# Routing attention and MLP mixer: the third pair's routing in PSUM bank 5, and softmax denominators finished two pairs at a time

## The chip, the cores and the metric

The kernel runs on one core of a Trainium2 chip. The metric is the device time of one execution in microseconds (us). The time before the change is 791.66 us, the median of three runs (791.56 to 792.14).

Five engines are spoken of: TensorE (PE, with its weight loads in rows of their own, PEld), VectorE (DVE), ScalarE (ACT), GpSimd (POOL) and SyncE (SP, which here only issues DMAs). TensorE writes its results to PSUM, eight banks of 2 KB for each of 128 partitions; all else lies in SBUF, in one array that the program calls `arena`.

## The reference

Four batches, eight heads, a sequence of 768 and 64 elements per head. Attention is limited to keys of the same cluster, and its output goes through an MLP mixer. Cut to what matters:

```python
B, H, S, D = q.shape                       # 4, 8, 768, 64
q_assign = argmax(q_n @ c_n.T); k_assign = argmax(k_n @ c_n.T)   # 16 centroids per head
mask = q_assign[:, :, :, None] == k_assign[:, :, None, :]
scores = np.where(mask, q @ k.T / sqrt(D), -1e9)
attn = exp(scores - max); attn = attn / (sum(attn) + 1e-9)
x = (attn @ v) as (B, S, H * D)            # (4, 768, 512)

xt = x.transpose(0, 2, 1)
h = np.maximum(xt @ w_tok1, 0.0) @ w_tok2  # d_tok = 256
u = x + h.transpose(0, 2, 1)
out = u + np.maximum(u @ w_ch1, 0.0) @ w_ch2   # d_ch = 1536
```

## The kernel before, in words

**How the order comes about.** The kernel first writes its whole work down as a list of operations with the engines that may do each, a cost for each engine, and keys for what it reads and writes (`Program.add`, L89): grains of SBUF, and PSUM banks as `("ps", n)`. `Program.plan` (L152) then makes one order out of it. TensorE's operations keep the order in which they were written down; each other engine takes, of what is ready, what is due first. Some operations have an earliest time: each of the 31 pieces of weights that DVE rounds may be loaded from 9 + 10 n us on (`START`, `STEP`, L1356). So a change of one cost, one key or one operation can move many instructions on all engines but TensorE.

**The attention stage.** The 32 heads are worked on as 16 pairs, four pairs to a batch; `pair(m)` (L1317) writes down one pair:

- `scores(m)` (L1161): 12 chunks. Chunk n writes banks 2s and 2s+1 with s = n % 3, one bank per head, so three chunks use banks 0 to 5 in turn. Each is a plain product in float32 and a mask product in bfloat16 added to it. ScalarE takes the exponential of each chunk out of PSUM (L1205).
- `join_qk`, `part_qk` and `load_qkr` prepare q and k of later pairs: ScalarE takes their 16-bit halves apart and joins them (L875), and SP's queue transposes them by DMA (L910).
- `route(m, bk)` (L1079): four matmuls of q and k against the centroids into bank `bk`, then on DVE a transpose out of that bank (L1098), a maximum (L1099), a comparison and a transpose back (L1103), and on ScalarE L1108, which makes the bfloat16 mask rows. They go through DRAM to form the mask M of the pair. Inside `pair(m)` stands `route(m + 2, 0)` for the pairs 1 to 13, into bank 0. The third pair's routing, `route(2, 0)`, is written down at the end of pair 0, behind `finish_x(0, 5, 0)` and thus right ahead of the scores of pair 1.
- `values(m, i)` (L1249): exp times v into banks 6 and 7, six steps, by the matmuls of L1238.
- `add_up(m)` (L1213): DVE adds the exponentials of a pair up (four additions of 1536 elements per partition, a fifth in ten of the pairs) for the denominators.
- `sums(m, bk)` (L1263): a product with ones gives the denominators in bank 5 (bank 4 for the last pair). It is called in the next pair, behind its second step of values.
- `finish_x(m, bk, part)` (L1278): part 0 transposes banks 6 and 7 into x (L1285). Part 1 transposes the denominators out of their bank into `denT` (L1292), clamps the 12 numbers (L1295), inverts them (L1302) and multiplies the 768 elements of the pair in x by them (a `tt`, L885).

**Fillers.** Between these DVE rounds the mixer's weights (`weight_round`, L1349: L1369, L1373, L1376, L1379 and a `tt`) and makes sums of them (`channel_weights`, L1426, which writes them to the DRAM array `wd`, L1487). TensorE does not need these until the mixer.

**The mixer.** Behind the last pair come `token1` (L1565), `token2` (L1610), `x_into_u` (L1652), and then the channel products (`product`, L1708), each split into seven half-size products, with sums before (`combine`, L1687, by DVE or GpSimd) and additions out of PSUM behind them by DVE. Meanwhile the weights are loaded once more and their range is checked (L1884, L1908).

**Helpers.** Most operations go through short helpers, so one line of the profile stands for many: `mm` L846 for matmuls, `copy` L865 and L867, `halves` L875, `tt` L885, `relu` L892, `dma` L905, `transpose` L910.

Of the kernel before, what the change touches and what calls it, by code (L numbers as in the profile page):

```python
# [14 lines left out]
ALU = mybir.AluOpType  # L15
# [3 lines left out]
B, H, S, D = 4, 8, 768, 64  # L19
C = 16  # L20
P = 128
NJ = S // P
# [8 lines left out]
HS = HJ * P  # L31
# [692 lines left out]
def kernel(  # L724
# [26 lines left out]
    nc = tc.nc  # L751
    g = Program()
    res = ctx.enter_context(ExitStack())
    arena = res.enter_context(tc.tile_pool(name="arena", bufs=1)).tile(
        [P, 206 * 256], F32, name="arena"
    )
    ps = res.enter_context(tc.tile_pool(name="ps", bufs=1, space=bass.MemoryType.PSUM)).tile(
        [P, 8, 512], F32, name="ps"
    )
# [8 lines left out]
    def buf(kb, shape, dt=F32):  # L768
        return Buf(arena, int(kb * 256), shape, dt)
# [10 lines left out]
    low = Buf(arena, 644, [1])  # L780
    wsum = Buf(arena, 704, [2, NWP])
    araws = [buf(at, [768, 2], U32) for at in (75, 3)]
    rcps = [Buf(arena, 384 + 32 * i, [2, NJ]) for i in range(2)]
    dall = Buf(arena, 448, [NP, 2, NJ])

    qks = [buf(3 + 6 * i, [2, NJ, 2, D]) for i in range(2)]
# [5 lines left out]
    msc0 = Buf(arena, 332, [2, 2])  # L792
    exs = [buf(48 + 6 * i, [2, S]) for i in range(6)] + [buf(96, [2, S])]
    es = [buf(84 + 6 * i, [2, S]) for i in range(2)]
    denT = buf(105, [HS])
    okb = buf(131.5, [HS])
    rt = [buf(106.5 + 1.5 * i, [HS]) for i in range(3)]

# [13 lines left out]
    xs = [buf(158 + 12 * b, [NJ, DM]) for b in range(B)]  # L812
# [27 lines left out]
    def bank(*i):  # L840
        return [("ps", n) for n in i]
# [41 lines left out]
    def tt(dst, a, b, op, n, rd, wr, engines=("DVE",)):  # L883
        def fn(e):
            (nc.vector if e == "DVE" else nc.gpsimd).tensor_tensor(out=dst, in0=a, in1=b, op=op)  # L885

        return g.add({e: cost(e, n) for e in engines}, fn, rd, wr)
# [10 lines left out]
    def vec(fn, c, rd, wr, early=0.0, after=0.0):  # L898
        return g.add({"DVE": c - 0.08}, lambda e: fn(), rd, wr, after=after, early=early)
# [36 lines left out]
    def load_v(m, after=0.0):  # L936
        b, hp = divmod(m, H // 2)
        t = vs[m % 3]
        dma(
            t.ap.rearrange("p h j d -> p h (j d)"),  # L940
            v[b, 2 * hp : 2 * hp + 2].rearrange("h (p j) d -> p h (j d)", p=P),
            [], t.k(), 384, 1536, after,
        )
# [92 lines left out]
    def turn_qk(m, banks, parts=range(3)):  # L1036
        src, T = qks[m % 2], Ts[m % 3]
        for n in parts:
            bk = banks[n]
            for i in range(4):  # L1040
                a, j = divmod(4 * n + i, NJ)
                a = 1 - a
                turn(
                    ps[:, bk, i * P : (i + 1) * P],
                    src.ap[:, a, j].rearrange("p h d -> p (h d)"),
                    [("qk", m % 2, a, 0), ("qk", m % 2, a, 1)] + src.rows(a, a + 1), bank(bk),
                )

            copy(
                T.ap[:, 4 * n : 4 * n + 4].rearrange("p a t -> p (a t)"), ps[:, bk], 512,  # L1050
                bank(bk), T.rows(4 * n, 4 * n + 4),
            )
# [15 lines left out]
    def join_qk(m):  # L1068

        T = Ts[m % 3]  # L1070
        dst = T.ap.bitcast(U16).rearrange("p a (t two) -> p a t two", two=2)
        for n in range(2):
            for r in range(0, NQK, NJ):
                halves(
                    dst[:, r : r + NJ, :, n], qkt[n].ap[:, r : r + NJ], S,
                    qkt[n].k() + [("exps", m - 2)], T.rows(r, r + NJ), kind="JOIN16",
                )
# [135 lines left out]
    def add_up(m):  # L1213
        st = unit[m]
        for n in range(2):
            a = es[n]
            x, y, z = st[HJ * n : HJ * n + HJ]
            tt(a.ap, x.ap, y.ap, ALU.add, 2 * S, x.k() + y.k(), a.k())
            tt(a.ap, a.ap, z.ap, ALU.add, 2 * S, a.k() + z.k(), a.k())
        a, b = es[1], es[0]  # L1220
        if FOLD[m] == "V":
            tt(a.ap, a.ap, b.ap, ALU.add, 2 * S, a.k() + b.k(), a.k())
        if FOLD[m] != "T":
            return

        def fn(e):
            nc.gpsimd.dma_start(
                a.ap.rearrange("p h t -> p (h t)"), b.ap.rearrange("p h t -> p (h t)"),
                accum_op=ALU.add,
            )  # L1230

        g.add({"POOL": 1.0}, fn, a.k() + b.k(), a.k(), (2.2 * 768 * 1024, 6144))
# [16 lines left out]
    def values(m, i):  # L1249
        V, ex = vs[m % 3], unit[m][i]  # L1250
        mms(
            [
                (
                    ps[32 * gr : 32 * gr + 32, 6 + h, c * HS // 2 : (c + 1) * HS // 2],
                    V.ap[:, h, i, 32 * c : 32 * c + 32], tokens(ex.ap[:, h], gr),
                    i == 0 and c == 0, i == NJ - 1, (0, 32 * gr),
                )
                for h in range(2) for c in range(2) for gr in range(4)
            ],
            1.29, V.k() + ex.k(), bank(6, 7), (P, 32),  # L1260
        )

    def sums(m, bk):  # L1263
        first = 0 if FOLD[m] == "-" else 1
        for n in range(first, 2):
            mms(
                [
                    (
                        ps[32 * gr : 32 * gr + 32, bk, 0:HS], ones.ap,
                        tokens(es[n].ap.rearrange("p h t -> p (h t)"), gr), n == first, n == 1,  # L1270
                        (0, 32 * gr),
                    )
                    for gr in range(4)
                ],
                0.645, es[n].k() + ones.k(), bank(bk), (P, 32),
            )

    def finish_x(m, bk, part):  # L1278
        b, hp = divmod(m, H // 2)
        x, rcp = xs[b], rcps[m % 2]  # L1280
        cols = slice(hp * P, (hp + 1) * P)
        xk = x.rows(0, NJ, hp * P, (hp + 1) * P)
        if part == 0:
            vec(
                lambda: nc.vector.transpose(  # L1285
                    out=x.ap[:, :, cols].rearrange("p j (c d) -> p c j d", d=32),
                    in_=ps[:, 6:8, 0:HS],
                ),
                0.96, bank(6, 7), xk,
            )  # L1290
            return
        vec(lambda: nc.vector.transpose(out=denT.ap, in_=ps[:, bk, 0:HS]), 0.57, bank(bk), denT.k())  # L1292

        def den():
            nc.vector.tensor_scalar(  # L1295
                out=dall.ap[:, m].rearrange("p h j -> p (h j)"),
                in0=denT.ap.rearrange("p (n r) -> p n r", r=32)[:, :, 0],
                scalar1=SUM_LO / 2, scalar2=2 * SUM_HI, op0=ALU.max, op1=ALU.min,
            )

        vec(den, 0.2, denT.k(), [("dall", m)])
        vec(lambda: nc.vector.reciprocal(out=rcp.ap, in_=dall.ap[:, m]), 0.2,  # L1302
            [("dall", m)], rcp.k())
        xv = x.ap[:, :, cols].rearrange("p j (h d) -> p j h d", h=2)
        tt(
            xv, xv,
            rcp.ap.rearrange("p h j -> p j h").unsqueeze(3).to_broadcast([P, NJ, 2, D]),
            ALU.mult, S, xk + rcp.k(), xk,
        )

    def next_qk(m):
        if m + 3 < NP:
            part_qk(m + 3)
            if m + 4 < NP:
                load_qkr(m + 4)

    def pair(m):  # L1317
        scores(m)
        if m >= 1 and m + 2 < NP:
            join_qk(m + 2)  # L1320
        if m:
            next_qk(m)
        for i in range(NJ):
            if i == 3 and m == 0:
                turn_qk(2, (1, 2, 3))
            if i == 4 and 1 <= m < NP - 2:
                route(m + 2, 0)
            if i == 1:
                if m:
                    sums(m - 1, 5)  # L1330
                    finish_x(m - 1, 5, 1)
                add_up(m)
            values(m, i)
        if m == NP - 1:
            sums(m, 4)
        finish_x(m, 5, 0)
        if m == NP - 1:
            finish_x(m, 4, 1)
        if m == 0:
            load_v(2)  # L1340
            route(2, 0)
            next_qk(m)
        if m + 3 < NP:
            load_v(m + 3)
# [620 lines left out]
    for m in range(NP):  # L1965
        pair(m)
# [78 lines left out]
```

## Time and profile before

| what | value |
|---|---|
| median of three runs | 791.66 us |
| profiled execution | 791.57 us |
| its span in the trace | 789.7 us |
| mean granted TensorE clock | 0.998 |
| PE busy | 778.3 us (99%) |
| DVE busy | 677.9 us (86%) |
| ACT busy | 460.5 us (58%) |
| POOL busy | 190.1 us (24%) |
| PEld busy | 462.6 us (59%) |
| moved by DMA | 143.68 MB, 182 GB/s in the mean |

The span is the time from the first to the last instruction in the trace; the execution's own time has 1.9 us more. "Busy" is the time in which an engine carries out an instruction other than register, branch, semaphore and DMA-issuing ones. In a row of the timeline stand the start, the duration, the engine, the line of the kernel, the operation, what it writes and reads, and how many instructions of one kind the row takes together; in brackets the idle time ahead of it and what ended it. Rows of groups have a total and a mean in ns. SPq is SP's queue of DMA issues.

### The profile page before, as it was taken

Reading aid. Unit: us, or ns where it says so; the run is one execution under the profiler, and the core shown is the slowest. Engines: PE = TensorE matmul, PEld = TensorE weight load, DVE = VectorE, ACT = ScalarE, POOL = GpSimd, SP = SyncE. Lnnn points to the kernel's source line nnn. Section 1 sums busy time; section 2 is a strip of 40 time slices with the busy share of each in tenths; the row PEclk is TensorE's granted clock in tenths of the full one; section 3 lists DMA queues with packets and bytes.
Section 4 is the critical chain, followed back from the end, with each engine's and each line's share of the span. In section 5 each row is a group of like instructions: output and inputs, shape, how many; then the busy total and the mean of one; then the engine's idle time right before and its main releaser. Section 6 shows DMA issues by size and latency. Waiting matters only on the chain.

```text
span 789.7 us, 15348 instructions
## 1 busy us (share of the span) xinstructions
PE 778.3 (99%) x5975; PEld 462.6 (59%) x5975; DVE 677.9 (86%) x876; ACT 460.5 (58%) x612; POOL 190.1 (24%) x185
## 2 busy tenths in 40 slices
PE   8999999999999999999999999999999999999996
PEld 5666666666666666545555555555555555555554
DVE  7889999999999999999999877999953577799964
ACT  6688888888889875598614368723235204400422
POOL 0000000000000000001273598600285289830000
PEclk9999999999999999999999999999999999999999
DMA  9776769876788944469849999966687844444667
GB/s 252 171 185 180 180 148 227 212 198 172 193 220 224 276 148 151 90 141 215 189 111 259 332 246 286 293 153 137 157 191 172 174 101 101 102 106 102 160 151 173
DMA packets 326576, 143.68 MB, mean 182 GB/s; under 512 B 260192, under 2 KB 322400, under 8 KB 326496
## 3 DMA queue, kind: packets, MB, share of 16 engines
q1 hardware_dynamic: 324128, 141.83, 71.7%
q8 instruction: 49, 0.80, 0.4%
q10 hardware_dynamic: 2368, 0.79, 0.4%
q14 instruction: 31, 0.25, 0.1%
HBM read 91.95 MB, written 28.61 MB: 153 GB/s over the span
## 4 chain that ended last, share of the span: by engine, by line
PE 86%; DVE 9%; issue 2%; ACT 2%; DMA 1%; SPq 0%; DVEq 0%
PE ps L846 69%; PE ps L1238 17%; DVE arena L885 7%; ACT arena L875 1%; DMA arena<-in_q_dram 1%; ACT arena L865 0%; DMA arena<-wd 0%; DVE arena L1285 0%; DVE arena L1373 0%; SPq L905 0%; DVE arena L1292 0%; DVE arena L1379 0%; ACT arena L892 0%; DVE arena L867 0%; SPq L910 0%
## 5 line engine op out<-in xcount | busy, mean ns | idle before, releaser
L846 PE MATMUL ps<-arena 128*128 128x384 f32 (+5 forms) x2727 | 640.7, 463 | 5.6 <-POOL arena masks.py:199 1.4
L846 PEld LDWEIGHTS ps<-arena 128*128 128x128 f32 (+2 forms) x2343 | 339.7, 184 | 252.3 <-issue 60.5
L885 DVE TENSOR_TENSOR arena<-arena 128x1536 f32<-128x1536 f32 (+6 forms) x350 | 372.6, 1084 | 9.8 <-PE ps L1238 2.6
L885 POOL TENSOR_TENSOR arena<-arena 128x384 f32<-128x384 f32 x179 | 189.4, 1088 | 507.4 <-DVE arena L885 380.9
L885 DVE TENSOR_TENSOR arena<-ps,arena 128x384 f32<-128x384 f32 (+3 forms) x227 | 189.2, 844 | 77.5 <-PE ps L846 75.2
L875 ACT COPY arena<-arena 128x768 uint16<-128x768 uint16 x221 | 189.0, 960 | 65.1 <-DMA arena<-arena 33.3
L1205 ACT ACTIVATE arena<-ps 128x768 f32<-128x768 f32 x192 | 150.6, 811 | 38.4 <-PE ps L846 36.8
L1238 PE MATMUL ps<-arena 128*32 128x192 f32 (+1 forms) x3248 | 144.9, 335 | 0.0
L1238 PEld LDWEIGHTS ps<-arena 128*32 128x32 f32 x3248 | 103.7, 110 | 44.1 <-issue 15.6
L865 ACT COPY arena<-ps 128x512 f32<-128x512 f32 (+2 forms) x42 | 30.3, 730 | 120.1 <-PE ps L846 117.8
L892 ACT ACTIVATE arena<-arena 128x1152 f32<-128x1152 f32 (+1 forms) x38 | 40.0, 1078 | 53.9 <-DVE arena L885 53.5
L1901 ACT ACTIVATE arena<-arena 128x768 f32<-128x768 f32 x40 | 38.7, 970 | 24.8 <-DMA arena<-in_moe_w_ch_dram 18.0
L846 PEld LDWEIGHTS <-arena 64*128 64x128 bf16 x384 | 19.2, 94 | 24.6 <-issue 0.2
L1373 DVE SCALAR_TENSOR_TENSOR arena<-arena 128x512 uint32<-128x512 uint32 (+1 forms) x31 | 21.1, 694 | 0.4
L1379 DVE SCALAR_TENSOR_TENSOR arena<-arena 128x512 f32<-128x512 uint32 (+1 forms) x31 | 20.0, 671 | 0.4
L1108 ACT ACTIVATE arena<-arena 128x384 bf16<-128x384 f32 x16 | 11.2, 701 | 12.0 <-issue 12.0
L1369 DVE TENSOR_SCALAR arena<-arena 128x512 uint32<-128x512 uint32 (+1 forms) x31 | 12.3, 408 | 4.1 <-DMA arena<-in_moe_w_tok_dram 4.1
L1285 DVE STREAM_TRANSPOSE arena<-ps 128x768 f32<-128x768 f32 x16 | 15.2, 952 | 0.4 <-PE ps L1238 0.4
L1376 DVE TENSOR_SCALAR arena<-arena 128x512 uint32<-128x512 uint32 (+1 forms) x31 | 13.5, 461 | 0.2
L1292 DVE STREAM_TRANSPOSE arena<-ps 128x384 f32<-128x384 f32 x16 | 9.3, 581 | 3.0 <-PE ps L1238 2.6
L867 DVE COPY arena<-ps 128x384 f32<-128x384 f32 (+2 forms) x11 | 7.0, 639 | 4.6 <-PE ps L846 4.6
L1098 DVE STREAM_TRANSPOSE arena<-ps 128x384 f32<-128x384 f32 x16 | 9.1, 571 | 1.7 <-PE ps L846 1.5
(57 smaller groups left out, 53.0 us busy)
## 6 DMA issues: line engine op xcount, KB each, us to landing
arena<-wd SPq DMA_DIRECT2D x196, 192.0 KB, 3.0
wd<-arena SPq DMA_DIRECT2D x84, 224.0 KB, 2.8
arena<-in_moe_w_ch_dram SPq DMA_DIRECT2D x96, 128.0 KB, 3.3
arena<-in_moe_w_ch_dram SPq DMA_DIRECT2D x16, 768.0 KB, 5.7
arena<-in_v_dram SPq DMA_DIRECT2D x16, 384.0 KB, 4.7
out_dram<-arena SPq DMA_DIRECT2D x14, 384.0 KB, 3.5
arena<-in_k_dram SPq DMA_DIRECT2D x13, 384.0 KB, 4.0
arena<-in_q_dram SPq DMA_DIRECT2D x13, 384.0 KB, 4.3
```

Of the source, the lines that this page charges most:

```text
L846: nc.tensor.matmul(dst, lhsT=lhsT, rhs=rhs, start=start, stop=stop, tile_position=pos, is_transpose=tr, skip_group_check=True,)
L865: nc.scalar.copy(out=dst, in_=src)
L875: nc.scalar.copy(out=dst, in_=src)
L885: (nc.vector if e == "DVE" else nc.gpsimd).tensor_tensor(out=dst, in0=a, in1=b, op=op)
L892: nc.scalar.activation(out=dst, in_=src, func=ACT.Relu)
L1205: lambda e, ex=ex, s=s, u=u: nc.scalar.activation(out=ex.ap[:, :, u * HS : (u + 1) * HS], in_=ps[:, 2 * s : 2 * s + 2, 0:HS], func=ACT.Exp ...
L1238: nc.tensor.matmul(dst, lhsT=lhsT, rhs=rhs, start=start, stop=stop, tile_position=pos, skip_group_check=True,)
L1285: lambda: nc.vector.transpose(out=x.ap[:, :, cols].rearrange("p j (c d) -> p c j d", d=32), in_=ps[:, 6:8, 0:HS],),
L1373: vec(lambda: nc.vector.scalar_tensor_tensor(out=TT, in0=hi, scalar=0xC0000000, in1=hh, op0=ALU.bitwise_and, op1=ALU.bitwise_or), 0.14 + 0 ...
L1376: vec(lambda: nc.vector.tensor_scalar(out=hh, in0=TT, scalar1=0xFF800000, scalar2=None, op0=ALU.bitwise_and), f, T.k(), h.k())
L1379: vec(lambda: nc.vector.scalar_tensor_tensor(out=ll, in0=lo, scalar=float(2.0**-52), in1=hh.bitcast(F32), op0=ALU.mult, op1=ALU.mult,), 0. ...
L1901: lambda e, i=i, func=func, bias=bias, n=n, hi=hi: nc.scalar.activation(out=hi, in_=hi, func=func, bias=bias, accum_out=wsum.ap[:, i, n : ...
```

## The change

Three things are changed. The third pair's routing writes bank 5 instead of bank 0. Part 1 of `finish_x` only transposes for a pair with an even number, into its half of a `denT` that is twice as large; for a pair with an odd number it also clamps, inverts and multiplies for both pairs, 24 denominators and 1536 elements. For that `denT` moves from 105 to 102 KB of each partition in `arena`, where `M0`, the mask of the first pair, lies before it (3 KB), and `rcps` doubles. The diff:

```diff
-    rcps = [Buf(arena, 384 + 32 * i, [2, NJ]) for i in range(2)]
+    rcps = [Buf(arena, 384 + 32 * i, [2, 2, NJ]) for i in range(2)]
...
-    denT = buf(105, [HS])
+    denT = buf(102, [2, HS])
...
     def finish_x(m, bk, part):
         b, hp = divmod(m, H // 2)
-        x, rcp = xs[b], rcps[m % 2]
+        x = xs[b]
         cols = slice(hp * P, (hp + 1) * P)
         xk = x.rows(0, NJ, hp * P, (hp + 1) * P)
         if part == 0:
...
             return
-        vec(lambda: nc.vector.transpose(out=denT.ap, in_=ps[:, bk, 0:HS]), 0.57, bank(bk), denT.k())
+        vec(
+            lambda: nc.vector.transpose(out=denT.ap[:, m % 2], in_=ps[:, bk, 0:HS]), 0.57,
+            bank(bk), denT.rows(m % 2, m % 2 + 1),
+        )
+        if m % 2 == 0:
+            return
+        rcp = rcps[m // 2 % 2]
+        cols = slice((hp - 1) * P, (hp + 1) * P)
+        xk = x.rows(0, NJ, (hp - 1) * P, (hp + 1) * P)
 
         def den():
             nc.vector.tensor_scalar(
-                out=dall.ap[:, m].rearrange("p h j -> p (h j)"),
-                in0=denT.ap.rearrange("p (n r) -> p n r", r=32)[:, :, 0],
+                out=dall.ap[:, m - 1 : m + 1].rearrange("p m h j -> p (m h j)"),
+                in0=denT.ap.rearrange("p m (n r) -> p (m n) r", r=32)[:, :, 0],
                 scalar1=SUM_LO / 2, scalar2=2 * SUM_HI, op0=ALU.max, op1=ALU.min,
             )
 
-        vec(den, 0.2, denT.k(), [("dall", m)])
-        vec(lambda: nc.vector.reciprocal(out=rcp.ap, in_=dall.ap[:, m]), 0.2,
-            [("dall", m)], rcp.k())
-        xv = x.ap[:, :, cols].rearrange("p j (h d) -> p j h d", h=2)
+        dk = [("dall", m - 1), ("dall", m)]
+        vec(den, 0.22, denT.k(), dk)
+        vec(
+            lambda: nc.vector.reciprocal(out=rcp.ap, in_=dall.ap[:, m - 1 : m + 1]), 0.24, dk,
+            rcp.k(),
+        )
+        xv = x.ap[:, :, cols].rearrange("p j (h d) -> p j h d", h=4)
         tt(
             xv, xv,
-            rcp.ap.rearrange("p h j -> p j h").unsqueeze(3).to_broadcast([P, NJ, 2, D]),
-            ALU.mult, S, xk + rcp.k(), xk,
+            rcp.ap.rearrange("p m h j -> p j (m h)").unsqueeze(3).to_broadcast([P, NJ, 4, D]),
+            ALU.mult, 2 * S, xk + rcp.k(), xk,
         )
...
         if m == 0:
             load_v(2)
-            route(2, 0)
+            route(2, 5)
             next_qk(m)
```

## The prediction

> **What bounds the kernel now.** I read the page first, then the busy time of each engine by stage, then TensorE's timeline, because a mean over the span hides which engine each stage waits for.
>
> ```profile
> span 789.7 us, 15348 instructions
> ...
> PE 86%; DVE 9%; issue 2%; ACT 2%; DMA 1%; SPq 0%; DVEq 0%
> ```
>
> The chain that ended last is matmuls, with some VectorE (DVE) work in it. By stage (each cell is busy us and the count of instructions):
>
> ```profile
> core 0: us, PE busy (x) PEld busy (x) DVE busy (x) ACT busy (x) POOL busy (x), PEclk, DMA share, GB/s
> ...
> 32.00:317.00 285.00, 284.07 (x4068) 176.24 (x4064) 269.43 (x370) 233.94 (x308) 0.00 (x0) 1.00 0.74 195
> 317.00:346.00 29.00, 28.99 (x232) 14.77 (x225) 28.57 (x32) 20.30 (x27) 0.00 (x0) 1.00 0.45 87
> 346.00:400.00 54.00, 52.72 (x147) 26.79 (x146) 51.77 (x101) 40.41 (x52) 12.04 (x12) 1.00 0.89 201
> ```
>
> In the attention stage (32 to 317) TensorE is busy 284.07 of 285 us and DVE 269.43, so DVE has some 15 us over. From 317 to 400 DVE is busy 80.3 of 83 us, and TensorE's gaps are there. TensorE's timeline shows these gaps:
>
> ```profile
> 31.78 0.83 PE L846 MATMUL ps<-arena 128*32 128x384 f32 x8
> 33.54 9.96 PE L846 MATMUL ps<-arena 64*128 64x384 f32 x72 [0.93 <-DVE arena L1098]
> ...
> 53.34 9.96 PE L846 MATMUL ps<-arena 64*128 64x384 f32 x72
> ...
> 72.45 10.16 PE L846 MATMUL ps<-arena 64*128 64x384 f32 x72
> ...
> 351.81 40.26 PE L846 MATMUL ps<-arena 128*128 128x512 f32 x112 [0.17 <-ACT arena L865]
> 392.57 6.72 PE L846 MATMUL ps<-arena 128*128 128x384 f32 x20 [0.50 <-DVE arena L885]
> 399.76 383.29 PE L846 MATMUL ps<-arena 128*128 128x384 f32 x1191 [0.47 <-DVE arena L885]
> ```
>
> Three things are to be seen: one wait of 0.93 us at 33.54; score blocks of 9.96 or 10.16 us with no gap for all the pairs after it; and waits for DVE up to 399.76, behind which TensorE runs to 783. So a gain has to survive the stage from 317 to 400, where DVE sets the pace.
>
> **The change part by part.** *Bank 5 for the third pair's routing.* The matmuls at 31.78 end with those of route(2, 0), and the next scores want bank 0 again, so they wait for L1098 to read it:
>
> ```profile
> 32.03 0.98 DVE L1285 STREAM_TRANSPOSE arena<-ps 128x768 f32<-128x768 f32 x1 [0.37 <-PE ps L1238]
> ...
> 32.94 0.54 DVE L1098 STREAM_TRANSPOSE arena<-ps 128x384 f32<-128x384 f32 x1
> ```
>
> With bank 5 the first scores (banks 0 and 1) start at once. What is late next is the third chunk, which writes banks 4 and 5. A pair's 12 chunks take 9.96 us, 0.83 each, so that chunk comes 1.66 us behind a start at 32.61, at 34.27. L1098 ends at 33.48 and keeps its place right behind L1285 in DVE's order of the changed program: no wait is left. Gain 0.93 us; nothing hides it, since TensorE has no other gap until 351.
>
> *Denominators of two pairs at once.* These are the durations (count, then busy us, mean ns):
>
> ```profile
> L885 DVE TENSOR_TENSOR arena<-arena 128x1536 f32<-128x1536 f32 x90 | 156.5, 1748 | 5.5 <-PE ps L1238 2.6 <-ACT arena L1205 0.3
> ...
> L1302 DVE RECIPROCAL arena<-arena 128x12 f32<-128x12 f32 x16 | 3.5, 226 | 0.4
> ...
> L1295 DVE TENSOR_SCALAR arena<-arena 128x12 f32<-128x12 f32 x16 | 2.3, 142 | 0.0
> ```
>
> ```profile
> 94.15 0.96 DVE L885 TENSOR_TENSOR arena<-arena 128x768 f32<-128x768 f32 x1
> ```
>
> Removed: 16 clamps (2.3 us), 16 reciprocals (3.5 us), 16 multiplies of 768 (16 x 0.96 = 15.4 us), 21.2 us in all. Added: 8 multiplies of 1536, which no row shows with a broadcast operand. The bounds are 1.75 us (the plain addition of that size) and 1.92 us (two of the old ones); I take 1.75, since the row at 94.15 shows the broadcast of 768 at the same 1.1 to 1.25 ns per element. Also added are 8 clamps and 8 reciprocals of 24 elements, between the price of 12 and double it; I take 0.15 and 0.30 us. That is 8 x 2.20 = 17.6 us, so DVE loses 3.6 us of work, with bounds of 4.3 and 0 (21.2 less 8 x (1.75 + 0.142 + 0.226), and nothing if every merged operation costs double). By the Trainium skill's "Vector Engine (DVE) Microarchitecture Reference", 5.2 Measured stream behaviour on trn2, a built-in operation costs 1.0417 ns per column and some 75 ns besides; by that a clamp or reciprocal of 12 would take an estimated 87 ns, where the rows have 142 and 226 for these short ones, so the rows decide; by the rule the tail below would save about 0.23 us instead of 0.40 and the sum be 791.3. Before 317 this is worth nothing by itself: TensorE does not wait for DVE there, and DVE itself waits for TensorE at its sums:
>
> ```profile
> DVE arena L1292 <- PE ps L1238: 2.6, 6, 1.4
> ```
>
> Every second pair gets 2.2 us where it had 1.3, the others none. The extra 0.9 us could push L1292, the additions and L1098 behind it in the pairs that route ahead. There L1098 is done 0.63 us before TensorE wants the bank:
>
> ```profile
> 129.19 0.58 DVE L1098 STREAM_TRANSPOSE arena<-ps 128x384 f32<-128x384 f32 x1
> ```
> ```profile
> 130.40 10.16 PE L846 MATMUL ps<-arena 64*128 64x384 f32 x72
> ```
>
> The planner answers with the filler, the rounding of weights: in the changed order the pairs with a double multiply hold less of it ahead of L1292 and the others more. I cost this at nothing; the cover is that 0.63 us per pair.
>
> *The order around it.* ScalarE's L1108 stands between the exponentials of nine pairs (as at 79.99), whose scores take 10.16 us and hold nine waits of the weight loads for L1205; where it stands ahead of all twelve (at 53.69) they take 9.96:
>
> ```profile
> PEld ps L846 <- ACT arena L1205: 4.3, 9, 0.5
> ```
> ```profile
> 53.69 0.71 ACT L1108 ACTIVATE arena<-arena 128x384 bf16<-128x384 f32 x1 [2.33 <-issue]
> ...
> 73.57 6.52 ACT L1205 ACTIVATE arena<-ps 128x768 f32<-128x768 f32 x8 [2.70 <-PE ps L846]
> 79.99 0.70 ACT L1108 ACTIVATE arena<-arena 128x384 bf16<-128x384 f32 x1
> ```
>
> In the changed order one of the nine, the scores of the tenth pair, has it ahead: 0.20 us. So TensorE reaches the last pair 1.13 us earlier.
>
> *Where DVE sets the pace.* The weight pieces have fixed earliest times in the planner, so with TensorE earlier, less of them fits ahead of the last pair's additions:
>
> ```profile
> 314.15 0.69 DVE L885 TENSOR_TENSOR arena<-arena 128x512 f32<-128x512 f32 x1
> 314.87 0.69 DVE L1373 SCALAR_TENSOR_TENSOR arena<-arena 128x512 uint32<-128x512 uint32 x1
> 317.12 12.23 DVE L885 TENSOR_TENSOR arena<-arena 128x1536 f32<-128x1536 f32 x10 [1.56 <-PE ps L1238]
> 329.27 0.58 DVE L1292 STREAM_TRANSPOSE arena<-ps 128x384 f32<-128x384 f32 x1
> 329.88 0.17 DVE L1295 TENSOR_SCALAR arena<-arena 128x12 f32<-128x12 f32 x1
> 330.16 0.58 DVE L1292 STREAM_TRANSPOSE arena<-ps 128x384 f32<-128x384 f32 x1
> ...
> 355.77 0.69 DVE L885 TENSOR_TENSOR arena<-arena 128x512 f32<-128x512 f32 x1 [0.66 <-DMA wd<-arena]
> ```
>
> The start at 317.12 waits for TensorE, so it moves 1.13 us ahead. In the tail one clamp goes (0.28 us from 329.88 to 330.16), the merged multiply saves 2 x 0.96 - 1.75 = 0.17, the longer clamp and reciprocal give back about 0.05: 0.40 us. But the two operations at 314.15 and 314.87 stand behind the additions in the changed order: 1.38 us more in the stage that is bound by DVE. The operation at 355.77, which was ready at 355.11, is thus reached at 355.11 - 1.13 - 0.40 + 1.38 = 354.96. It overwrites a buffer that three writes to DRAM read, and SP's queue holds these writes between transposes:
>
> ```profile
> 352.56 1.06 SPq L905 DMA_DIRECT2D wd<-arena  x2
> 353.72 1.25 SPq L910 DMA_TRANSPOSE arena<-arena  x1
> ...
> 356.68 1.22 SPq L910 DMA_TRANSPOSE arena<-arena  x1
> ```
>
> Before, the third write went out at 353.09 (352.56 and half of 1.06) and DVE went on 2.68 us later. In the changed order two writes stand ahead of this transpose and the third behind it. The transpose follows ScalarE's copies and moves up with them (1.1 to 1.5 us): 352.3, and 1.25 us for it, then 2.68: 356.2. DVE waits 1.2 us there instead of 0.66 and goes on 0.43 us later than before. The bounds: no growth of the wait (DVE at 354.96) and one more transpose ahead of the third write (2.96 us more, 353.72 to 356.68 being the step of the queue there).
>
> From there to 399.76 the order holds the same filler in sum, but two DVE halves of a subtraction went to GpSimd, one ahead of that point:
>
> ```profile
> 396.00 0.91 DVE L885 TENSOR_TENSOR arena<-arena 128x384 f32<-128x384 f32 x1
> ```
>
> That takes 0.91 us from DVE. Its reader comes 21 matmuls behind the start at 399.76, some 7 us later (383.29 us / 1191 = 0.32 us each), which covers GpSimd's slower pace.
>
> **Sum:** +0.43 - 0.91 = -0.48 at the wait of 399.76, behind which TensorE runs without DVE. The profiled execution took 791.57 us (span 789.7 and 1.9 around it), 0.09 below the median of 791.66, so the forecast is **791.1 us**.
>
> **The rivals.** *The write is not late* (faster). If the wait of 0.66 does not outlast 354.96, DVE goes on 0.81 us earlier than before, and with 0.91 that is 1.72: 789.9 us. For it speaks that SP's queue moves up as a whole; against it that the third write has a transpose ahead of it. Chance 0.23.
>
> *DVE's saved work counts in full* (faster). If DVE were the engine that bounds all stages, the 3.6 us would come on top of the 0.93: 787.0 us. Against it stand the waits of L1292 for TensorE. Chance 0.02. The Trainium skill's "Perfetto Trace Analysis", Identifying the Most-Contended Engine, ranks VectorE by its occupancy and calls matmul busy time no good measure of headroom, which would favour this rival; the stage row 32:317, with TensorE short of 0.93 us only, does not bear it out.
>
> *The write is later still* (slower). In SP's queue the third write is issued in order; if its transpose waits for ScalarE until the next one's time, the write lands 2.96 us later than in my sum and every us of that is one of DVE's: 794.1 us. It decides from about 2.1 us beyond 356.2, that is 358.3, where the kernel is 0.2% slower than before. For it: DVE has no slack there. Against: the transposes before 353.72 follow ScalarE, which moves up. Chance 0.14, the pairs that use up the 0.63 us included.
>
> *The wait only moves* (the change does not do what it says). If L1098 fell behind filler, the third chunk would wait on bank 5 as the first did on bank 0: 0.93 us back, 792.0 us. The order of DVE speaks against it. Chance 0.06.
>
> **How the numbers follow.** A measurement can tell about 0.2% from no change here, 1.58 us: below 790.08 is faster, above 793.24 slower. The forecast has 0.55 and lies within, as does the fourth case (together 0.61); faster has 0.25, slower 0.14. The range reaches down past the first rival and up past the fourth: 789.5 to 792.8, which leaves out the slower case and the full gain of DVE, with a little of the edges.
>
> **What would show it.** In the profile after: no wait for L1098 at 33 us; scores of the tenth pair at 9.96 us; multiplies of 1536 near 1.75 us; the last additions on DVE begin near 316.0; the wait of DVE for the write to DRAM near 355 to 356 at about 1.2 us; TensorE's last wait for DVE near 399.3. Wrong would be: any wait of TensorE for DVE between 36 and 317, or TensorE's last wait below 398.5 or above 401.

## The result and the profile after

The changed kernel takes 789.62 us (median of eight runs, 789.11 to 790.05) against 791.61 us for the kernel before (eight runs, 791.01 to 792.14). The ratio is 0.9975 with a 95% interval from 0.9966 to 0.9985: about 2.0 us faster, between 1.2 and 2.7. The forecast of 791.1 us was 1.5 us too high; the time lies in its range, 0.1 us above its lower end, and nearest to the first rival (789.9 us, the write is not late). It is below the 790.08 us from which the prediction spoke of "faster", a case to which it gave 0.25.

The profiled execution after took 789.87 us with a span of 788.0 us. The page's chain that ended last has lost most of VectorE:

```profile
span 788.0 us, 15324 instructions
...
PE 95%; DVE 3%; DMA 1%; issue 0%; ACT 0%; SPq 0%
```

Before, DVE had 9% of that chain. By stage, with the columns of the same view of before (busy us and count for PE, PEld, DVE, ACT, POOL):

```profile
32.00:317.00 285.00, 285.00 (x4092) 177.02 (x4088) 266.44 (x349) 234.40 (x309) 0.00 (x0) 1.00 0.74 194
317.00:346.00 29.00, 29.00 (x225) 14.72 (x218) 28.72 (x30) 21.27 (x28) 0.00 (x0) 1.00 0.52 106
346.00:400.00 54.00, 53.43 (x149) 27.37 (x148) 51.85 (x102) 39.55 (x51) 14.34 (x14) 1.00 0.83 201
```

TensorE is busy 285.00 of 285 us up to 317 (284.07 before) and 53.43 of 54 us from 346 to 400 (52.72 before). Its timeline:

```profile
32.30 10.72 PE L846 MATMUL ps<-arena 128*32 128x384 f32 x80
...
187.86 9.96 PE L846 MATMUL ps<-arena 64*128 64x384 f32 x72
...
206.98 10.16 PE L846 MATMUL ps<-arena 64*128 64x384 f32 x72
...
324.66 67.10 PE L846 MATMUL ps<-arena 128*128 128x512 f32 x174
391.92 6.07 PE L846 MATMUL ps<-arena 128*128 128x384 f32 x18 [0.15 <-DVE arena L885]
398.30 11.23 PE L846 MATMUL ps<-arena 128*128 128x384 f32 x34 [0.31 <-DVE arena L885]
410.02 371.42 PE L846 MATMUL ps<-arena 128*128 128x384 f32 x1157 [0.48 <-DVE arena L885]
```

The 80 matmuls at 32.30 are the eight that stood at 31.78 and the 72 of the scores in one row: no gap is left between them. One more block of scores (187.86) takes 9.96 us. The waits at 351.81 and 392.57 are gone or shorter, and there is a new one of 0.48 us at 410.02.

**A ruler for two traces.** Every trace here has 5975 matmul records in the same order, so the start of the nth can be compared between kernels. One offset has to be taken out first. The 31st record is the first that waits for q from DRAM, and nothing before it differs between these kernels, but it starts at different times. The row of before, then that of after:

```profile
6.75 0.95 PE L846 MATMUL ps<-arena 128*128 128x128 f32 x7 [0.46 <-DMA arena<-in_q_dram]
```
```profile
7.26 0.95 PE L846 MATMUL ps<-arena 128*128 128x128 f32 x7 [0.70 <-DMA arena<-in_q_dram]
```

In the twelve traces of this table it lies between 6.75 and 7.76 us. The table gives, counted from that record, how much earlier (minus) or later the same matmul starts than in the trace of before, in us. The columns are named by the times of before.

| kernel | 33.54 | 351.81 | 399.76 | 410.83 | 555.01 | last (783.64) | median us, ratio to before with interval |
|---|---|---|---|---|---|---|---|
| changed kernel | -0.99 | -1.48 | -1.97 | -1.32 | -2.01 | -2.11 | 789.62, 0.9975 (0.9966 to 0.9985) |
| e6_bank_order | -1.00 | -1.01 | -1.02 | -1.02 | -1.03 | -1.02 | 790.94, 0.9992 (0.9983 to 1.0001) |
| e7_den_order | 0.00 | -0.12 | +0.13 | +0.13 | +0.14 | +0.14 | 791.60, 1.0000 (0.9991 to 1.0009) |
| e8_both_order | -1.00 | -1.12 | -1.12 | -1.12 | -1.25 | -1.24 | 790.66, 0.9988 (0.9979 to 0.9997) |
| e4_bank0 | -1.02 | -0.69 | -1.17 | -0.54 | -1.23 | -1.33 | 790.56, 0.9991 (0.9982 to 1.0000) |
| e1_bank | -1.00 | -0.93 | -1.32 | -0.50 | -1.05 | -1.04 | 790.60, 0.9987 (0.9978 to 0.9996) |
| e2_den | -0.03 | -0.31 | -0.17 | +0.42 | -0.47 | -0.56 | 790.98, 1.0004 (0.9983 to 1.0024) |
| e3_split | -1.02 | -1.55 | -2.03 | -1.39 | -2.09 | -2.18 | 789.71, 0.9975 (0.9964 to 0.9985) |
| e10_copies | -1.02 | -1.16 | -1.17 | -1.17 | -1.30 | -1.30 | 790.66, 0.9987 (0.9978 to 0.9996) |
| e11_halves | -1.00 | -1.13 | -1.42 | -0.64 | -0.84 | -0.84 | 790.58, 0.9988 (0.9979 to 0.9997) |
| e12_moved | -1.03 | -2.85 | -3.35 | -2.72 | -0.62 | -0.72 | 788.64, 0.9959 (0.9946 to 0.9973) |

Each row is one profiled execution; the medians are of all runs of the same kernel, the profiled one among them, and have their own spread. By the medians alone some gains are at the edge of what the interval tells (e6: 0.9983 to 1.0001); there the hundredths rest on one trace each.

### The profile page after: what moved, and what is told of

It is laid out like the page before. It is cut to its first block, busy times and chain, and to the rows that moved or that the text cites. A ratio compares the mean times of both kernels' runs of the same rounds, so it can differ in the third digit from the quotient of the medians.

```text
span 788.0 us, 15324 instructions
## 1 busy us (share of the span) xinstructions
PE 777.8 (99%) x5975; PEld 463.1 (59%) x5975; DVE 675.2 (86%) x848; ACT 461.4 (59%) x614; POOL 194.1 (25%) x187
## 4 chain that ended last, share of the span: by engine, by line
PE 95%; DVE 3%; DMA 1%; issue 0%; ACT 0%; SPq 0%
PE ps L846 77%; PE ps L1238 18%; DVE arena L885 2%; DMA arena<-in_q_dram 1%; DMA arena<-in_moe_w_ch_dram 0%; ACT arena L865 0%; DVE arena L1384 0%; DVE arena L1390 0%; DVE arena L1387 0%; SPq L905 0%; DVE arena L1380 0%; DVE arena L867 0%; ACT arena L1129 0%
## 5 line engine op out<-in xcount | busy, mean ns | idle before, releaser
L885 POOL TENSOR_TENSOR arena<-arena 128x384 f32<-128x384 f32 x181 | 193.4, 1109 | 501.8 <-DVE arena L885 378.6
L1108 ACT ACTIVATE arena<-arena 128x384 bf16<-128x384 f32 x16 | 11.2, 701 | 13.6 <-issue 13.6
L1098 DVE STREAM_TRANSPOSE arena<-ps 128x384 f32<-128x384 f32 x16 | 9.1, 571 | 1.8 <-PE ps L846 1.8
L1103 DVE STREAM_TRANSPOSE arena<-arena 128x384 f32<-128x384 f32 x16 | 9.3, 578 | 0.6
```

## The experiments

Two questions were open: which part of the change gives the time, and whether it does so by its work or by the order that the planner makes of it. For the first four kernels the plan was kept and only what the planned instructions do was changed.

**e6_bank_order, e7_den_order, e8_both_order: the two parts in the order of before.** The planner sees the kernel before. In e6 route(2) then uses bank 5; in e7 an even pair's clamp, reciprocal and multiply are left out and the odd pair's do both; e8 has both edits.

```diff
 e6:
-                ps[32 * gr : 32 * gr + 32, bk, 0:HS], cbd.ap[:, hp],
+                ps[32 * gr : 32 * gr + 32, 5 if m == 2 else bk, 0:HS], cbd.ap[:, hp],
 e7:
+        def inv():
+            if m % 2:
+                nc.vector.reciprocal(out=rcp.ap, in_=dall.ap[:, m - 1 : m + 1])
...
-        vec(lambda: nc.vector.reciprocal(out=rcp.ap, in_=dall.ap[:, m]), 0.2,
+        vec(inv, 0.2, [("dall", m)], rk)
```

> The order of the kernel before on every engine, with route(2) physically in bank 5: only the wait of 0.93 us at 33.54 can go. Theory A (the wait is the gain, and DVE, which between 317 and 400 starts when TensorE hands over its last values, passes it on): TensorE enters the last pair 0.9 to 1.0 us earlier and keeps all of it, about 790.7 us. Rival B (the gain is VectorE's saved work): no change, 791.6. Rival C (the gain is the new order): no change that lasts, the wait of 0.66 us for the write to DRAM at 355.77 grows and eats it, 791.2 to 791.6.

> The order of the kernel before, routing in bank 0, but clamp, reciprocal and multiply of a pair with an even number are left to the next pair and done for both at once: 3.5 us of VectorE work less and nothing else moved. Theory A: nothing up to 317, 0.4 us in the tail behind the last additions, so about 791.2 us. Rival B: VectorE's 3.5 us count in good part, 789.6 or less. Rival C: no change, 791.6.

> Both parts in the order of the kernel before. Theory A: the sum of the two, 0.95 + 0.4, so 790.2 to 790.4 us, with the 0.2 us of the scores of the tenth pair and what the new order does behind 346 still missing against the changed kernel. Rival B: as the denominators alone. Rival C (the order makes the gain): 791.2 or more.

Measured: e6 wins 1.00 us at the second pair's scores and still has 1.02 at the end. e7 has won nothing (+0.14 in the trace, 791.60 us). e8 has 1.24, that is 0.22 more than e6. So the wait on bank 0 is worth its full price, and VectorE's saved work nothing by itself and at most 0.22 us beside bank 5: e7 has VectorE busy 295.02 us from 32 to 346 where before has 297.99, and the time is the same. Two places in e7 show why. The first is one pair whose cover of 0.63 us was used up by the double multiply (VectorE, then TensorE):

```profile
207.43 0.58 DVE L1099 STREAM_TRANSPOSE arena<-ps 128x384 f32<-128x384 f32 x1
```
```profile
208.06 10.16 PE L847 MATMUL ps<-arena 64*128 64x384 f32 x72
```

The routing's transpose of the bank ends at 208.01, right where the scores start, and the same matmul comes 0.16 us later than in before. The second is the wait for the write to DRAM, in the list of VectorE's waits from 317 to 412:

```profile
DVE arena L886 <- DMA wd<-arena: 1.2, 1, 1.2
```

It was 0.66 us before: what VectorE saved behind the last additions, it waits for the write.

**e4_bank0: the wait put back into the changed kernel.** Planned as bank 5, issued on bank 0, so every engine keeps the order of the changed kernel. In this order the first matmul of the next scores is issued ahead of L1098, so the third pair's mask is made from scores, not from the routing.

```diff
-                ps[32 * gr : 32 * gr + 32, bk, 0:HS], cbd.ap[:, hp],
+                ps[32 * gr : 32 * gr + 32, bk if m != 2 else 0, 0:HS], cbd.ap[:, hp],
```

> The changed kernel in its own order on every engine, but route(2) physically writes and reads bank 0 again: the wait of TensorE for L1098 comes back. Theory A: 0.93 to 1.0 us slower than the changed kernel, about 790.6 us. Rival B and rival C: the changed kernel's time, 789.6 to 789.9, because the wait is made up for in a stage that VectorE sets.

```profile
32.23 1.67 PE L846 MATMUL ps<-arena 128*32 128x384 f32 x12
34.58 9.22 PE L846 MATMUL ps<-arena 64*128 64x384 bf16 x68 [0.67 <-DVE arena L1098]
```

The wait is back, behind the first few score matmuls and with 0.67 us. The last matmul is 0.78 us later than in the changed kernel (2.11 less 1.33), the median 0.94. A wait at 34 us goes through to the end here too.

**e1_bank and e2_den: one part each, with an order of its own.** e1 is the kernel before with `route(2, 5)`, e2 the changed kernel with `route(2, 0)`.

> Only route(2) in bank 5, and the planner makes its own order. The theory as it stands after the runs in the order of before (the wait is worth 0.9 to 1.0 us, the rest of the gain of 2 us is the order that the planner found): TensorE 1.0 us earlier from 33 us on; in all 790.7 us if this order is as good as that of before, and anything between 789.6 and 791.6 by the order behind 346. Rival (the two parts need each other): 791.2 or more.

> Only the denominators of two pairs at once, routing in bank 0, and the planner makes its own order. The theory (the merged work is worth nothing by itself, the order is what counts): the wait of 0.93 us stands at 33 us, and the time is 791.6 us less what this order gives, 790.6 to 791.8. Rival (it is the merged work that lets VectorE pass on TensorE's lead): 789.8 or less is impossible without the bank, so 790.6 and the merged work visible as fewer waits of TensorE for VectorE behind 380.

e1 gains 1.04 us in the trace, as much as e6 does at the end: its own order is worth nothing over that of before. e2 gains 0.56 where e7, with the same work in the order of before, lost 0.14: the order that the planner makes of the merged operations is worth 0.70. The interval of e2's ratio (one of its eleven runs took 799.83 us) is too wide to say so by the times.

**e3_split: the order of the changed kernel, the operations of each pair issued apart.**

```diff
+        def inv():
+            for n in range(2):
+                nc.vector.reciprocal(out=rcp.ap[:, n], in_=dall.ap[:, m - 1 + n])
...
-            lambda: nc.vector.reciprocal(out=rcp.ap, in_=dall.ap[:, m - 1 : m + 1]), 0.24, dk,
+        vec(inv, 0.24, dk, rcp.k())
```

> The changed kernel in its own order on every engine, but each merged clamp, reciprocal and multiply is issued as two, one per pair: VectorE's 3.5 us of work are back, the order is kept. The theory (they lie in VectorE's slack up to 317, and only the 0.4 us behind the last additions can show): 789.9 to 790.2 us, with up to 0.3 us per pair where the second multiply stands ahead of L1098 and uses up its 0.63 us. Rival (VectorE's saved work is the gain): 791.0 or more.

The time is that of the changed kernel (789.71 and 789.62 us), and the lead is within 0.1 us of it in every column. But the experiment put less work back than I expected. VectorE's rows in e3, then in the changed kernel:

```profile
151.27 0.21 DVE L1304 TENSOR_SCALAR arena<-arena 128x12 f32<-128x12 f32 x2
151.43 0.31 DVE L1315 RECIPROCAL arena<-arena 128x12 f32<-128x12 f32 x2
151.70 1.83 DVE L1323 TENSOR_TENSOR arena<-arena 128x768 f32<-128x768 f32 x2
```
```profile
151.18 0.14 DVE L1303 TENSOR_SCALAR arena<-arena 128x24 f32<-128x24 f32 x1
151.36 0.30 DVE L1312 RECIPROCAL arena<-arena 128x24 f32<-128x24 f32 x1
151.70 1.76 DVE L885 TENSOR_TENSOR arena<-arena 128x1536 f32<-128x1536 f32 x1
```

From the start of the clamp to the end of the multiply e3 takes 2.26 us and the changed kernel 2.28. From 32 to 346 VectorE is busy 295.55 and 295.17 us, 0.4 more in e3, not 3.5. So e3 does not test VectorE's work; e7 and e8 do. What e3 shows is that bank 5 and the order of the changed kernel repeat the time, whether its operations are issued merged or apart.

**e10_copies and e11_halves: two moves of the new order, each alone.** The plans of before and after differ in the engine of four operations ahead of 560 us: two copies out of PSUM (516.0 and 541.4) went from VectorE to ScalarE, and two halves of a subtraction (396.0 and 400.1) from VectorE to GpSimd. Each kernel is e8 with one of these pairs issued as in the changed kernel.

```diff
-            o.fn(e)
+            o.fn({2885: "ACT", 2975: "ACT"}.get(o.seq, e))      (e10)
+            o.fn({2522: "POOL", 2525: "POOL"}.get(o.seq, e))    (e11)
```

> Both parts in the order of the kernel before, but the two copies out of PSUM that VectorE made at 516.0 and 541.4 us are ScalarE's, as in the changed kernel; nothing else is moved. Theory (these copies delayed VectorE's additions behind 516, and so TensorE at 521.8 and 555.0): these two waits of 0.24 and 0.33 us go, 790.1 us against 790.66 with the copies on VectorE. Rival (the waits come from the other moves of the new order): 790.66.

> Both parts in the order of the kernel before, but the two halves of a subtraction that VectorE did at 396.0 and 400.1 us are GpSimd's, as in the changed kernel; nothing else is moved. Theory by the term of the prediction: 0.91 us less on VectorE ahead of 399.76, so TensorE is there 0.6 to 0.9 us earlier and keeps it, 789.9 us. Rival (VectorE and GpSimd disturb each other, and TensorE waits at 410 instead): the lead is lost again by 411 us, 790.4 to 790.9.

e10: no change against e8 (-1.30 and -1.24 at the end, 790.66 us both). The copies alone are not what made TensorE wait at 521.8 and 555.0; that theory fell. e11: TensorE is 0.30 us earlier at 399.76, and then loses 0.78 up to 410.83, so it ends 0.40 later than e8 in the trace; the medians (790.58 and 790.66) do not tell the two apart. VectorE in e8, then in e11:

```profile
404.06 0.68 DVE L1383 SCALAR_TENSOR_TENSOR arena<-arena 128x512 uint32<-128x512 uint32 x1
404.78 1.11 DVE L1386 TENSOR_SCALAR arena<-arena 128x512 uint32<-128x512 uint32 x1
405.92 0.69 DVE L1389 SCALAR_TENSOR_TENSOR arena<-arena 128x512 f32<-128x512 uint32 x1
406.65 1.47 DVE L886 TENSOR_TENSOR arena<-arena 128x512 f32<-128x512 f32 x1
408.48 1.36 DVE L886 TENSOR_TENSOR arena<-ps,arena 128x1152 f32<-128x1152 f32 x1 [0.36 <-PE ps L847]
```
```profile
404.42 1.49 DVE L1383 SCALAR_TENSOR_TENSOR arena<-arena 128x512 uint32<-128x512 uint32 x1
405.94 0.43 DVE L1386 TENSOR_SCALAR arena<-arena 128x512 uint32<-128x512 uint32 x1
406.40 1.37 DVE L1389 SCALAR_TENSOR_TENSOR arena<-arena 128x512 f32<-128x512 uint32 x1
407.81 1.37 DVE L886 TENSOR_TENSOR arena<-arena 128x512 f32<-128x512 f32 x1
409.10 2.61 DVE L886 TENSOR_TENSOR arena<-ps,arena 128x1152 f32<-128x1152 f32 x2
```

The first four operations take 3.95 us in e8 and 4.66 in e11; the three additions ahead of them, from 401 us on, take 2.71 and 3.50. In e8 the addition out of PSUM behind them waits 0.36 us for TensorE; in e11 it starts 0.62 us later and waits for nothing: TensorE waits for it.

**e5_late, e9_behind, e12_moved: ScalarE's L1108 behind the twelve exponentials.** The eight blocks of 10.16 us that are left in the changed kernel promise 8 x 0.2 = 1.6 us. e5 makes L1108 due 12 us later from the fourth pair on; e9 lets it wait for the pair's last exponential; e12 takes the planned order of the changed kernel and moves L1108, with the DMAs of the mask, behind that exponential for the masks of pairs 4 to 12.

```diff
 e5:
+            early=-12.0 if m >= 3 else 0.0,
 e9:
+        if masks:
+            rest, n = masks.pop()
+            rest([("exps", n)])
 e12:
+            n = next(i for i, (o, e) in enumerate(order) if o.mode == ("rows", m))
+            last = max(i for i, (o, e) in enumerate(order) if o.mode == ("exp", m - 1))
...
+            order[n : last + 1] = stay + moved
```

> The changed kernel with a due time 12 us later for L1108 of the pairs from the fourth on, so that ScalarE takes it behind the twelve exponentials and not among them. If the 0.2 us of every pair with a score block of 10.16 us is L1108 among the exponentials, eight such blocks fall to 9.96 and TensorE reaches the last pair 1.6 us earlier. Theory (the lead is passed on, as the 1.0 us of bank 5 was): 788.0 to 788.6 us. Rival (VectorE's fillers, bound to their loads, do not get done in the shorter time): the blocks fall to 9.96, but TensorE waits as much more for VectorE between 346 and 420, 789.6.

> The changed kernel, but from the fourth pair on L1108 is written down behind the scores of the pair in which it is carried out, and waits for their last exponential; the routing's work on VectorE keeps its due times. ScalarE then has the twelve exponentials in one go in every pair. Theory: nine score blocks at 10.16 us (eight of them here) fall to 9.96, the masks still land 2 us or more before they are wanted, and TensorE's lead of 1.6 us at the last pair is passed on like that of bank 5: 788.0 to 788.4 us. Rival 1: the masks come late as they did with the later due time, and TensorE waits for them in every pair: over 790. Rival 2: VectorE, with less time for its fillers, gives the lead back between 346 and 420: 789.6.

> The changed kernel with its own order on TensorE, VectorE and GpSimd; for the masks of pairs 4 to 12 alone, L1108 is moved behind the last exponential of the pair in which it stands, with the DMAs that carry the mask. Theory: the eight score blocks of 10.16 us fall to 9.96, and since these masks are not the one that came late when all were moved, the 1.6 us reach the last pair; VectorE's order is that of the changed kernel, and its idle time up to 317 lets it keep up: 788.0 to 788.4 us. Rival (VectorE, whose fillers stand in the same order, needs the time): TensorE's waits for VectorE between 346 and 412 grow by what was won, 789.6.

e5 takes 822.84 us, 31 us slower than the kernel before. The due time is passed on to what L1108 depends on, so VectorE's routing came late as well, and the masks after it. From its list of waits:

```profile
ACT arena L1108 <- DVE arena L1103: 22.3, 6, 7.3
PE ps L846 <- DMA arena<-wdm: 21.9, 8, 5.9
```

e9 takes 793.84 us (ratio 1.0027, 1.0018 to 1.0036). All blocks up to there fall to 9.96 us, and from 237 us on (in the times of before) TensorE is 1.5 us ahead of the changed kernel. Then the mask of one pair, at 267 us, is late, and TensorE waits for it:

```profile
PE ps L846 <- DMA arena<-wdm: 2.3, 1, 2.3
```

The wait is 2.3 us, but some 4.3 us are gone, for TensorE's clock falls behind it (the stages of e9; the clock stands third from the end):

```profile
264.00:266.70 2.70, 0.51 (x4) 0.00 (x0) 2.63 (x6) 0.00 (x0) 0.00 (x0) 1.00 1.09 191
266.70:269.00 2.30, 2.22 (x12) 1.49 (x14) 2.30 (x2) 1.50 (x2) 0.00 (x0) 0.79 1.15 280
269.00:271.20 2.20, 2.20 (x11) 1.45 (x9) 2.13 (x5) 0.94 (x2) 0.00 (x0) 0.50 1.01 360
271.20:274.00 2.80, 2.80 (x22) 2.08 (x21) 2.70 (x7) 2.39 (x3) 0.00 (x0) 0.96 0.93 363
```

Another 2 us are lost between 366 and 412, the stage of the second rival. So the first rival held in one pair and not in every pair.

e12 takes 788.64 us, 0.9959 of before (0.9946 to 0.9973). In its trace all blocks but one (10.19) take 9.96 us and the lead over the changed kernel is 1.4 us, kept through the stage of VectorE (-2.72 against -1.32 at 410.83), so its theory holds up to there. But this execution, 791.60 us and the slowest of five, then lost 2.9 us:

```profile
499.85 15.98 PE L860 MATMUL ps<-arena 128*128 128x384 f32 x48 [1.26 <-POOL arena L899]
516.60 266.73 PE L860 MATMUL ps<-arena 128*128 128x384 f32 x833 [0.77 <-ACT arena L879]
```

Two of the other runs took 787.55 and 787.61 us, 0.4 us below the range of the theory, two 788.64 and 789.12. e12 is faster than before; that it is faster than the changed kernel the intervals do not settle, and why it has these waits in some runs stays open.

## Why the prediction was right or wrong, step by step

Up to 317 us the mechanism was as forecast. Behind 346 us it was not, and there luck had a part: steps that were wrong in opposite senses came near to cancelling. The prediction's own sign of being wrong, a last wait of TensorE for VectorE above 401 us, did appear (410.02).

- **The wait on bank 0: right.** Forecast 0.93, measured 0.99 to 1.03 us in every kernel that has bank 5. The third chunk found bank 5 read: no wait took its place.
- **The work of the denominators: right in size, right in value.** Forecast 17.6 us in place of 21.2. The sizes in the page's groups of after:

```profile
L1312 DVE RECIPROCAL arena<-arena 128x24 f32<-128x24 f32 x8 | 2.4, 303 | 0.3
L1303 DVE TENSOR_SCALAR arena<-arena 128x24 f32<-128x24 f32 x8 | 1.2, 145 | 0.0
```

  With 8 multiplies at 1.76 these are 17.7 us. VectorE's busy time, in which rows that overlap count once, falls by 3.0 us in e7 and not by 3.6. That it is worth nothing up to 317 is what e7 shows. The cover of 0.63 us did not always hold in the order of before (0.16 us in one pair); in the planner's own order it held.
- **The tenth pair's block: right.** 9.96 us at 187.86.
- **The 791.3 us given beside the tail does not follow from the sum.** The tail's 0.40 us is a part of VectorE's arrival at 354.96, and the sum goes by the write, up to which VectorE waits (356.2). A tail of 0.23 us would have left it at 791.1.
- **The write to DRAM: wrong, and the largest term.** The step said that the third write lands late and VectorE goes on at 356.2, 0.43 us later than before. SP's queue in the trace of after:

```profile
351.89 1.25 SPq L910 DMA_TRANSPOSE arena<-arena  x1
353.18 0.58 SPq L905 DMA_DIRECT2D wd<-arena  x1
```

  The order was as foreseen, the third write behind one more transpose. But that transpose went at 351.89, which is 351.38 less the offset of 0.51 at the start, and not at 352.3: it moved up by 2.3 us, not by 1.4. And I had taken 2.68 us from issue to restart where the trace of before has the write issued at 353.18 and landed at 355.58, 2.40 us. In the trace of after it is issued at 353.18 and lands at 355.43, 2.25 us from its issue. VectorE:

```profile
355.15 0.42 DVE L1380 TENSOR_SCALAR arena<-arena 128x512 uint32<-128x512 uint32 x1
355.62 0.69 DVE L885 TENSOR_TENSOR arena<-arena 128x512 f32<-128x512 f32 x1
```

  It comes to the operation at 355.57, 0.14 us behind the landing, and goes on without a wait. Less the offset that is 355.06, where the sum had 354.96, so the arrival was right. The operation starts at 355.11, less the offset, and not at 355.77 as in before: the +0.43 became -0.66, and as to the write the first rival held. In the order of before (e8) the same operation still waits 0.70 us.
- **The halves on GpSimd: wrong in sign.** The step took 0.91 us from VectorE and called GpSimd's pace covered. e11 shows 0.30 us won at 399.76 and 0.78 lost by 410.83. The changed kernel has the same loss: -1.97 at 399.76, -1.32 at 410.83.
- **"Behind 399.76 TensorE runs without DVE": wrong.** The changed kernel has the wait at 410.02. And in before TensorE loses 0.24 us at 521.8 and 0.33 at 555.0 (in the ruler), which the changed kernel does not. At 555.0 the profile names an addition of VectorE that ends at 554.96. At 521.8 it names no releaser, but VectorE's rows differ, in before, then in after:

```profile
517.93 0.56 DVE L885 TENSOR_TENSOR arena<-ps,arena 128x384 f32<-128x384 f32 x1
518.41 2.81 DVE L885 TENSOR_TENSOR arena<-arena 128x1152 f32<-128x1152 f32 x2
521.14 0.55 DVE L885 TENSOR_TENSOR arena<-ps,arena 128x384 f32<-128x384 f32 x1
```
```profile
517.69 0.55 DVE L885 TENSOR_TENSOR arena<-ps,arena 128x384 f32<-128x384 f32 x1
518.16 1.35 DVE L885 TENSOR_TENSOR arena<-arena 128x1152 f32<-128x1152 f32 x1
519.43 0.55 DVE L885 TENSOR_TENSOR arena<-ps,arena 128x384 f32<-128x384 f32 x1
```

  In before two additions of 1152 elements stand between two additions out of PSUM, and the second of these ends at 521.69, 0.10 us ahead of TensorE's matmul at 521.79. That distance is 0.09 to 0.10 us in all six kernels with the order of before. In e10, one of them, the copy is gone, but VectorE then idles for 0.62 us and starts the first of the two additions out of PSUM at 517.35, 3.85 us ahead of the matmul, as in e8. In the changed kernel only one addition of 1152 stands between the two, the second ends at 519.98, and the same matmul starts at 520.61 without a gap; e1 to e4, e9 and e12, which have newly planned orders, have one there too and no gap. So for 521.8 the traces point to that one move; it was not tried alone, and what frees 555.0 stays open.
- **What the sum lacked: the order as a term of its own.** Both parts in the order of before give 1.24 us (e8), the changed kernel 2.11: 0.87 us come from the order. At 399.76 the changed kernel is 0.85 us ahead of e8, with the tenth pair's block (0.2) and the write found in time among the causes; by 410.83 only 0.20 us of this is left. The rest comes at 521.8, at 555.0 and right behind. So the time came near the 789.9 us of the first rival by luck: most of the lead at 399.76 was gone by 411 us, and waits that the prediction did not know of gave as much back when they went. The two copies (e10) and the two halves (e11), each tried alone, do not make the 0.87 us; the other moves were not tried alone.

The rival that VectorE's work counts in full is refuted by e7, the one that the wait only moves by e6.

## What to carry to other kernels

A wait that is alone on the bounding engine is worth its length at the end of the program, if nothing behind it waits for something that does not move along: here 1.0 us at 33 us was 1.0 us at 783 (e6). Work saved on an engine with slack was worth nothing by itself (3.0 us of VectorE's work in e7), but a scheduler that plans with it makes another order, and that can be worth as much as the edit (0.9 of 2.1 us here); plan the edit and issue the old work, or plan the old work and issue the edit, to tell the two apart. Where SP's queue carries a write that an engine waits for, take its issue and landing from the trace, and not the restart of the reader.

## What the runs showed of the hardware

- **A wait of 2.3 us on TensorE was followed by a lower clock, another of 2.9 us was not.** In the rows of e9 above the granted clock is 0.79, 0.50 and 0.96 in the three stretches behind the wait, and the wait costs 4.3 us instead of 2.3. The 0.67 us of e4 had no such tail (0.78 us in all). In e5 TensorE waits 2.92 us for a mask up to 167.73, and its clock stays at 1.00 in the wait and behind it:

```profile
164.80:167.70 2.90, 0.00 (x1) 0.00 (x0) 2.83 (x5) 0.80 (x2) 0.00 (x0) 1.00 1.03 244
167.70:170.00 2.30, 2.27 (x16) 1.58 (x18) 2.30 (x6) 1.57 (x2) 0.00 (x0) 1.00 0.92 153
```

  So the length of the wait alone did not decide it; what did, these runs do not show. The Trainium skill's "TensorE: Matmul & The Clock Gate", Part 1: The HAM clock gate, has the clock halve after an idle window of about 3.4 us; the halving is in the rows of e9, but there a shorter wait came before it.

- **VectorE beside GpSimd.** In the rows of e8 and e11 above, an operation of VectorE with all its operands in SBUF takes 0.68 us alone and 1.37 to 1.49 beside a GpSimd operation, or 0.43 and 1.11: some 0.7 to 0.8 us more each time. GpSimd's rows in e11 lie over the operation of 1.49 up to 405.37 and, from 406.15 on, over most of the two of 1.37; the one of 0.43 starts at 405.94, in the gap between them:

```profile
398.63 6.74 POOL L886 TENSOR_TENSOR arena<-arena 128x384 f32<-128x384 f32 x6 [0.51 <-PE ps L847]
406.15 2.48 POOL L886 TENSOR_TENSOR arena<-arena 128x384 f32<-128x384 f32 x2 [0.79 <-PE ps L847]
```

  The Trainium skill's "SBUF — State Buffer", SBUF: two separate sides, says of the port pair that VectorE and GpSimd share that it is locked for a whole instruction and the other engine blocks; these rows agree with a block of most of a 1.0 us GpSimd operation.
- **Two short operations without a dependence cost little more than one.** Two clamps of 12 take 0.21 us together and two reciprocals 0.31 (e3), where one alone has a mean of 0.142 and 0.226: the second adds 0.07 to 0.08. The Trainium skill's "Vector Engine (DVE) Microarchitecture Reference", 5.2 Measured stream behaviour on trn2, gives 1.0417 ns per column and some 75 ns per instruction, an estimated 87 ns for 12; for the second of two the rows agree, for one alone they are longer. For the reciprocal the agreement can be chance: one of 24 elements takes 303 ns, 77 more than one of 12 (226), where the clamp takes 145 and 142.
